# Linear attention whose matmuls all use TensorE tiles of 64 rows by 128 columns, on one Trainium2 core

## The chip, the cores and the metric

The kernel runs on one core of one Trainium2 chip. The core has TensorE (PE, with its weight loads shown apart as PEld), VectorE (DVE), ScalarE (ACT), GpSimd (POOL) and SyncE (SP, which here only issues DMAs). The metric is the time of one execution on the device in microseconds; less is better.

## The reference

Attention with exponential features for 8 batches of 8 heads, 576 tokens each, head size 64, followed by a mixture of experts (MoE) over the 4608 tokens. All is float32.

```python
def phi(x):
    proj = np.einsum('bhsd,df->bhsf', x, w_phi)                      # 128 features
    proj = proj - np.max(np.abs(proj), axis=-1, keepdims=True)
    return np.concatenate([np.exp(proj), np.exp(-proj)], axis=-1)    # 256 features
q_p, k_p = phi(q), phi(k)
kv  = np.einsum('bhsf,bhsd->bhfd', k_p, v)
z   = np.sum(k_p, axis=2)
num = np.einsum('bhsf,bhfd->bhsd', q_p, kv)
den = np.einsum('bhsf,bhf->bhs', q_p, z)[..., None] + 1e-06
x   = (num / den).transpose(0, 2, 1, 3).reshape(B * S, H * D)        # 4608 x 512
# MoE: logits = x @ w_gate; experts of equal capacity are filled in order of the logits;
# out[its tokens] = relu(x @ w1[e]) @ w2[e], for 8 experts, hidden size 1024
```

## The kernel before

Attention goes over 16 units, each two batches by two heads: 18 chunks of 128 tokens of one head, 9 for each of the two heads `a`. The two batches lie one behind the other, so of the 9 chunks four belong to the first batch, four to the second, and the one between them (`s_ == 4`, `j == 4`) is half and half. A unit's steps have names that the planner and this text use:

- `ld`: SyncE loads `ki`, `qi`, `vi` (L106 to L122), two to three units ahead.
- `kt`, `qt`: TensorE transposes k and q, 128 by 128 (L165, L243); ScalarE copies them out of PSUM (`kh`, `qh`).
- `kg`, `qg`: the projection on `w_phi` (`project`, L152), in tiles of 64 by 64: three groups of 12 matmuls for k and three for q. VectorE takes the largest absolute value of each token (`km`, `qm`, L156) and subtracts it (`kt`, `qtt`, L159). For k, ScalarE takes the two exponentials (`kP`, L177 and L178). For q, TensorE first transposes the difference (`T`, L255), so that features stand on partitions; then ScalarE takes the exponentials (`qP`, L258).
- `kv`: v stands still, `kP` moves, 64 columns by 256 features (L189, L194). GpSimd adds up `kP` over chunks (`ad`, L201 to L205), and TensorE sums that over tokens against a column of ones (`z`, L234).
- `bd`: the result is copied to `kvT` and multiplied by a block-diagonal matrix `bd` that holds a unit matrix and the gate weights (L222). This gives `kz`: per feature 64 columns of key-value, 8 of key-value times gate, and one for the key sum.
- `num`: `qP` stands still in tiles of 128 rows by 64 columns, `kz` moves, 73 columns (L279). VectorE adds 1e-6 to the denominator, inverts it, multiplies the 8 gate columns (`lg`, L288) and the 64 others (`xp`, L298). `xp` is stored to `xs` in DRAM, and the logits pile up in `L`.

At the end of each batch pair (every fourth unit) VectorE also does a first part of the routing (`pr`), and TensorE a count (`cnt`). After attention comes the routing, then the experts, whose rows are gathered from `xs`.

The order on each engine is written by the class `Plan`. Every step is an entry with an engine, a duration in ns, a due time, the steps it depends on, and claims on buffers (`slot`); PE steps also carry the tile shape (`mode`: A 128 by 128, B 128 by 64, Q 64 by 64). `order` repeatedly takes the engine's cheapest candidate; the resulting order is fixed, and each engine works through its own in order. In PSUM, two tiles `D` of two banks each serve `kg`, `qg`, `T` and `bd`; two tiles `S` of one bank serve `kt`, `qt`, `z`, `num` and `cnt`; two banks belong to `kv`.

Of the kernel before, what the change touches and what calls it, by code (L numbers as in the profile page):

```python
# [17 lines left out]
class Plan:  # L18
# [3 lines left out]
    SEM=40.; dl=0.; wp=6.  # L22
# [5 lines left out]
    def order(self):  # L28
# [7 lines left out]
        while left:  # L36
            best=None; horizon={}
            cand={}
            for x in left:
                e=x['eng']  # L40
                if len(cand.get(e,()))>=40: continue
                r=x['after']
                ok=x['seq'] is None or 'start' in self.by[x['seq']]
                if not ok: continue
                for d_ in x['deps']:
                    y=self.by[d_]
                    if 'end' not in y: ok=False; break
# [25 lines left out]
            if e=='PE':  # L73
                m0=x['mode'][0]
                if mode[0] not in (None,m0): s+=95.
                if mode[0]!=m0 or s>free.get(e,0.)+1.: s+=100. if m0=='A' else 50.
# [13 lines left out]
def attention(ctx, tc, nc, q, k, v, w_phi, w_gate, xs, L, C, xp, cfg={}, after=None, later=None, count=None, init=iter(())):  # L90
# [3 lines left out]
    d=dict(TI=21.,kt=-4.,kg=0.,kv=4.,bd=4.,z=5.,zc=6.,qt=6.,qg=10.,T=2.5,num=26.,stay=2.,ks=4.,qs=4.,ns=5.,ng=6,ld=60.,nqP=8,init=25.,pitch=1.)  # L94
# [7 lines left out]
    p=ps.tile([128,512],F32,name='S0',bufs=1)  # L102
    for _ in range(cfg.get('nwarm',7)): PE.matmul(p,w[:,0:128],w,start=True,stop=True)
    T={}
    HS=S*D
    def load(u,first=lambda: None):  # L106
        bp,hp=divmod(u,NP)
        qi=sb.tile([128,2,9,D],F32,name='qi',bufs=2); ki=sb.tile([128,2,9,D],F32,name='ki',bufs=2); vi=sb.tile([128,2,9,D],F32,name='vi',bufs=3)
        T['q',u],T['k',u],T['v',u]=qi,ki,vi
        def put(t,p,s0,s1,x,b,row):  # L110
# [22 lines left out]
    KV=(((0,0),(1,5),(0,1),(1,6),(0,2),(1,7),(0,3),(1,8)),((0,9),(1,14),(0,10),(1,15),(0,11),(1,16),(0,12),(1,17)))  # L133
    dv=lambda n,ps_=True: (150 if ps_ else 110)+1.03*n-95
    ac=lambda n,ps_=True: (170 if ps_ else 200)+.83*n-100
    QI=227.
    def unit(u):
        bp,hp=divmod(u,NP)
        t0=u*d['TI']
        def add(name,eng,dur,due,fn,deps=(),mode=None,slot=(),frees=(),lat=None,after=0.):  # L140
            P.add((name,u),eng,dur,t0+due,fn,[(x,u) for x in deps],
                  lat={'PE':170.,'DVE':95.,'ACT':100.,'POOL':30.,'SP':0.}[eng] if lat is None else lat,mode=mode,slot=slot,frees=frees,after=after)
        add('ld','SP',600. if u else 0.,-d['ld'],lambda x: load(u) if u else None,slot=(('qi',2,('qi',u)),('ki',2,('ki',u)),('vi',3,('vi',u))),lat=4500. if u else 0.)
        def slots(*l): return tuple((kd,n,(kd,u) if len(z)==0 else (kd,u)+tuple(z)) for kd,n,*z in l)
        ld0=('ld',)

        def project(x,X,src,i0,i1):
            p=X['p']=bank(X['b'],[128,2,512])(x)
            for i in range(i0,i1):
                for c in range(2):  # L150
                    for r in range(2):
                        PE.matmul(p[64*(c^r):64*(c^r)+64,r,128*(i-i0):128*(i-i0)+128],src[64*r:64*r+64,i,64*(c^r):64*(c^r)+64],C['w'][64*r:64*r+64,:],start=True,stop=True,skip_group_check=True)  # L152
# [8 lines left out]
        for g in range(3):  # L161
            def pe(x,g=g):
                if g==0: T['kh',u]=sb.tile([128,9,128],F32,name='kh',bufs=2)
                p=T['ktp',u,g]=bank(('S',u,'kt',g),[128,3,128])(x)
                for i in range(3): PE.transpose(p[:,i],ch(T['k',u],3*g+i),ident)  # L165
            def act(x,g=g): A.copy(T['kh',u][:,3*g:3*g+3],T['ktp',u,g])
            due=d['kt']+d['ks']*1.5*g
            add(('kt',g),'PE',327.,due,pe,ld0,'A',slots(('S',NS,'kt',g),*((('kh',2),) if g==0 else ())),(('ki',u),),after=(5500.,9000.,10000.)[g] if u==0 else 0.)
            add(('kh',g),'ACT',ac(384),due+.4,act,(('kt',g),),frees=(('S',u,'kt',g),))
        for g in range(3):  # L170
# [12 lines left out]
        for g in range(2):
            def pe(x,g=g):
                kP=T['kP',u]; v_=T['v',u]
                if g==0: T['kvps',u]=[ps.tile([128,256],F32,name='kv%d'%i,bufs=1) for i in range(2)]
                for i,b in KV[g]:
                    a,s_=divmod(b,9); c=a^i
                    PE.matmul(T['kvps',u][i][64*c:64*c+64,:],v_[:,a,s_,:],kP[:,b,:],start=b in (0,5,9,14),stop=False,skip_group_check=True)  # L189
                if g==1:  # L190
                    for a in range(2):
                        for i in range(2):
                            c=a^i; r=slice(64*i,64*i+64)
                            PE.matmul(T['kvps',u][i][64*c:64*c+64,:],v_[r,a,4,:],kP[r,9*a+4,:],start=False,stop=True,skip_group_check=True)  # L194
            add(('kv',g),'PE',4*430.+(530. if g==1 else 0.),d['kv']+d['ks']*(2+2.5*g),pe,[('ke',1+g)]+([('kv',0)] if g else []),('B','Q') if g else 'B',slots(('kv',1)) if g==0 else (),(('kP',u),('vi',u)))
        def ad(a,i):
            def f(x):
                kP=T['kP',u]
                if a==0 and i==0: T['ks',u]=sb.tile([128,2,2,256],F32,name='ks',bufs=2)
                ks=T['ks',u]; X=lambda s_: kP[:,9*a+s_:9*a+s_+6:5]  # L200
                if i==0: G.tensor_add(ks[:,:,a],X(0),X(1))  # L201
                elif i<3: G.tensor_add(ks[:,:,a],ks[:,:,a],X(i+1))  # L202
# [12 lines left out]
        def bdp(x):
# [674 lines left out]
```

## Time and profile before

| what | us |
|---|---|
| runs (median; all) | 858.12; 858.25, 856.98, 858.12 |
| the profiled execution | 857.9 |
| its span, first to last instruction | 856.1 |
| TensorE busy in the span | 803.4 |
| VectorE busy | 570.2 |
| ScalarE busy | 370.0 |
| GpSimd busy | 262.1 |

```profile
PEclk9999999999999999958999999999999999999999
```

The last line cuts the span into 40 slices of 21.4 us and gives the granted TensorE clock in tenths; it is full but for two slices behind the end of attention, where the routing keeps TensorE idle. A row of a timeline is start, length, engine, line, operation, output and inputs, tile (rows\*columns), moving operand, count, and in brackets the idle time before it with what ended it. A row of groups ends in the busy time, the mean ns of one, and the idle time before them. A row of stretches is the stretch, its length, the busy time of PE, PEld, DVE, ACT and POOL, the granted clock, the DMA share and GB/s.

### The profile page before, as it was taken

How to read it: one execution, taken by the hardware profiler on the slowest of the kernel's cores; microseconds unless marked ns; L12 is line 12 of the kernel's file. 1: busy time of each engine (PE TensorE's matmuls, PEld its weight loads, DVE VectorE, ACT ScalarE, POOL GpSimd, SP SyncE). 2: the span in 40 equal slices, each digit the busy share in tenths (PEclk: the TensorE clock that was granted, in tenths of full speed). 3: DMA queues.
4: the chain of work that ended last, by engine and by line, in shares of the span. 5: the costliest groups of instructions: out<-in, count | busy, mean ns of one | idle time of the engine just before them, and what ended most of it. 6: DMA issues, size and time to landing. Idle time of an engine off the chain costs nothing.

```text
span 856.1 us, 24776 instructions
## 1 busy us (share of the span) xinstructions
PE 803.4 (94%) x10508; PEld 685.8 (80%) x10508; DVE 570.2 (67%) x1534; ACT 370.0 (43%) x691; POOL 262.1 (31%) x300
## 2 busy tenths in 40 slices
PE   4879999999999999758999999999999999999995
PEld 2768887887788878658979879889889798898984
DVE  1787788778867887577858658668667577461410
ACT  1646665566566565413334324333333243251410
POOL 1654455555555555111040130310301202401001
PEclk9999999999999999958999999999999999999999
DMA  8424444454445421134143340532233225610301
GB/s 170 116 54 113 114 114 126 118 135 121 117 120 134 117 58 31 57 114 131 54 147 118 129 147 35 177 131 95 97 118 123 83 104 185 214 63 38 118 13 43
DMA packets 73534, 91.88 MB, mean 107 GB/s; under 512 B 5280, under 2 KB 56512, under 8 KB 73424
## 3 DMA queue, kind: packets, MB, share of 16 engines
q1 hardware_dynamic: 67328, 71.32, 29.3%
q0 software_dynamic: 6096, 18.98, 6.5%
q8 instruction: 83, 1.36, 0.7%
q14 instruction: 27, 0.22, 0.1%
HBM read 71.40 MB, written 18.87 MB: 105 GB/s over the span
## 4 chain that ended last, share of the span: by engine, by line
PE 69%; issue 16%; DVE 7%; POOL 4%; DMA 2%; ACT 1%; SPq 0%; POOLq 0%; DVEq 0%; ACTq 0%
PE h L763 19%; PE y L792 16%; PE S L279 7%; PE D L152 6%; PE kv L189 4%; PE D L255 3%; PE y L807 2%; PE S L165 2%; PE S L243 2%; PE h L739 2%; PE S L234 2%; DVE km L156 1%; PE rps L530 1%; POOL out_dram L821 1%; DVE kt L159 1%
## 5 line engine op out<-in xcount | busy, mean ns | idle before, releaser
L763 PE MATMUL h<-xh,w1h 128*128 128x272 f32 (+1 forms) x512 | 145.9, 305 | 0.7 <-ACT xh L740 0.7
L763 PE MATMUL h<-xh,w1l 128*128 128x304 f32 (+1 forms) x512 | 143.9, 301 | 0.0
L774 ACT ACTIVATE fh<-h 128x272 fp32r<-128x272 f32 (+1 forms) x128 | 49.2, 384 | 134.5 <-PE h L763 122.1
L821 POOL DMA_INDIRECT out_dram<-ysb,idx x40 | 40.5, 1012 | 207.0 <-ACT ysb L815 203.5
L792 PE MATMUL y<-w2h,fl 128*128 128x512 f32 x256 | 102.0, 398 | 0.0
L792 PE MATMUL y<-w2l,fh 128*128 128x512 f32 x256 | 101.9, 398 | 0.0
L792 PE MATMUL y<-w2h,fh 128*128 128x512 f32 x256 | 101.5, 396 | 0.0
L763 PEld LDWEIGHTS h<-xh,w1h 128*128 128x128 f32 x512 | 97.2, 190 | 2.5 <-issue 1.2
L763 PEld LDWEIGHTS h<-xh,w1l 128*128 128x128 f32 x512 | 97.4, 190 | 0.0
L734 POOL DMA_INDIRECT xg<-xs,idx x40 | 40.0, 1000 | 178.2 <-issue 141.5
L763 PE MATMUL h<-xl,w1h 128*128 128x272 f32 (+1 forms) x512 | 91.4, 298 | 0.0
L778 DVE SCALAR_TENSOR_TENSOR fl<-h,fh 128x272 fp32r<-128x272 f32 (+1 forms) x128 | 52.8, 419 | 55.6 <-ACT fh L774 41.9
L201 POOL TENSOR_TENSOR ks<-kP 128x512 f32<-128x512 f32 x32 | 40.9, 1277 | 157.1 <-issue 130.2
L279 PE MATMUL S<-kz,qP 128*64 128x73 f32 x2304 | 87.4, 230 | 1.0 <-ACT xp L296 1.0
L279 PEld LDWEIGHTS S<-kz,qP 128*64 128x64 f32 x2304 | 78.1, 137 | 11.0 <-issue 9.1
L202 POOL TENSOR_TENSOR ks<-ks,kP 128x512 f32<-128x512 f32 x64 | 81.5, 1273 | 4.9
L258 ACT ACTIVATE qP<-D 128x768 f32<-128x768 f32 x96 | 72.5, 808 | 9.1 <-PE D L255 5.6
L763 PEld LDWEIGHTS h<-xl,w1h 128*128 128x128 f32 x512 | 75.5, 188 | 0.0
L815 ACT COPY ysb<-y 128x512 f32<-128x512 f32 (+1 forms) x40 | 21.8, 544 | 104.4 <-PE y L792 72.3
L156 DVE TENSOR_REDUCE km<-D 128x6 f32<-128x768 f32 x48 | 45.7, 953 | 29.4 <-PE D L152 29.2
L189 PE MATMUL kv<-kP,vi 128*64 128x256 f32 x512 | 60.9, 379 | 0.0
L156 DVE TENSOR_REDUCE qm<-D 128x6 f32<-128x768 f32 x48 | 45.6, 950 | 20.0 <-PE D L152 19.8
(177 smaller groups left out, 1550.5 us busy)
## 6 DMA issues: line engine op xcount, KB each, us to landing
raww<-in_moe_w_dram SPq DMA_DIRECT2D x64, 512.0 KB, 5.5
qi<-in_q_dram SPq DMA_DIRECT2D x32, 288.0 KB, 4.6
xs<-xp SPq DMA_DIRECT2D x16, 576.0 KB, 3.8
ki<-in_k_dram SPq DMA_DIRECT2D x32, 160.0 KB, 3.8
vi<-in_v_dram SPq DMA_DIRECT2D x32, 160.0 KB, 5.2
ki<-in_k_dram SPq DMA_DIRECT2D x32, 128.0 KB, 3.7
vi<-in_v_dram SPq DMA_DIRECT2D x32, 128.0 KB, 5.0
xg<-xs,idx POOLq DMA_INDIRECT x40, 3.5
```

Of the source, the lines that this page charges most:

```text
L152: PE.matmul(p[64*(c^r):64*(c^r)+64,r,128*(i-i0):128*(i-i0)+128],src[64*r:64*r+64,i,64*(c^r):64*(c^r)+64],C['w'][64*r:64*r+64,:],start=True ...
L156: V.tensor_reduce(m[:,:,0:n],X['v'],axis=AX.X,op=OP.max,apply_absolute_value=True)
L189: PE.matmul(T['kvps',u][i][64*c:64*c+64,:],v_[:,a,s_,:],kP[:,b,:],start=b in (0,5,9,14),stop=False,skip_group_check=True)
L201: if i==0: G.tensor_add(ks[:,:,a],X(0),X(1))
L202: elif i<3: G.tensor_add(ks[:,:,a],ks[:,:,a],X(i+1))
L258: for fh in range(2): A.activation(qP[:,fh].rearrange('p (b i) f -> p b (i f)',b=2),X['T'][:,:,0:384],AF.Exp,scale=1.0-2*fh)
L279: PE.matmul(p[64*ab:64*ab+64,j-j0,:],T['qP',u,jj][:,fh,o,64*ab:64*ab+64],T['kz',u][:,ab,fh,a^ab,:],start=fh==0,stop=fh==1)
L763: PE.matmul(p,ws[:,k,o:o+128],xx[:,k,o1:o2],start=n==0,stop=n==11)
L774: A.activation(hh[:,f,o1:o1+m1],p[:,0:m1],AF.Relu)
L778: V.scalar_tensor_tensor(hl[:,f,o1:o1+m1],p[:,0:m1],0.0,hh[:,f,o1:o1+m1],op0=OP.max,op1=OP.subtract)
L792: PE.matmul(p,hx[:,f,o:o+128],ws[:,f%2,:],start=n==0,stop=n==23)
L821: st=G.indirect_dma_start(out=ov,out_offset=bass.IndirectOffsetOnAxis(ap=iv,axis=0),in_=yv,in_offset=None)
```

## The change

All of attention's matmuls and transposes take tiles of 64 rows by 128 columns; two such tiles (`r` = 0 and 1, rows 0 to 63 and 64 to 127) write to two different PSUM banks.

- `project`: a chunk takes two matmuls instead of four.
- `turn` replaces the 128 by 128 transposes of k, q and the difference by two of 64 rows and 64 moving columns each. k and q come in groups of 3 and 6 chunks.
- `kv`: `kP` stands still (128 features), and `v1`, v with a column of ones, moves (65 columns); the key sum is the 65th column, so `ad` and `z` go. GpSimd makes `v1` (`vc`). The halves of the tokens land in two banks: ScalarE copies the first to `kz` (`kc`), VectorE adds the second (`kd`).
- The gate columns: both heads' key-value is transposed (`kT`, 4 pairs), copied, and multiplied by the gate weights `gw` (`gt`, 8 matmuls of 8 columns); VectorE copies the result to `kz` (`zk`).
- `num`: the sum over 128 feature rows is split over two banks. ScalarE copies bank 0 to `nu` (`xc`), VectorE adds bank 1 (two additions where the group has the mixed chunk, whose product is 146 columns wide), then as before, on `nu` in SBUF. The multiplication of the 64 columns goes to GpSimd (`xa`), in the last unit too, where ScalarE did it.
- All PSUM tiles of attention come from one ring of four tiles of two banks.
- q is laid out like k and v, in four loads instead of two, each of k, q and v has a planner entry of its own, and the rows of `xs` are stored by four DMAs instead of one; the table of token numbers follows (four iotas for one).
- The planner counts several claims of one kind, and a table `off` sets the due time of each step (`o0` and `oL` shift those of the first and last unit).

```diff
-                for c in range(2):
-                    for r in range(2):
-                        PE.matmul(p[64*(c^r):64*(c^r)+64,r,128*(i-i0):128*(i-i0)+128],src[64*r:64*r+64,i,64*(c^r):64*(c^r)+64],C['w'][64*r:64*r+64,:],start=True,stop=True,skip_group_check=True)
+                for r in range(2): PE.matmul(p[:,r,128*(i-i0):128*(i-i0)+128],src[64*r:64*r+64,i,:],C['w'][64*r:64*r+64,:],start=True,stop=True,skip_group_check=True)
...
+    ND_=4
+    def bank(u_):
+        return lambda x: ps.tile([128,2,512],F32,name='D%d'%x['buf'][u_],bufs=1)
+    def turn(p,n,f):
+        for i in range(n):
+            for r in range(2): PE.transpose(p[:,r,64*i:64*i+64],f(i)[64*r:64*r+64,:],ident[64*r:64*r+64,64*r:64*r+64])
...
+        def vcopy(x):
+            v1=T['v1',u]=sb.tile([128,2,9,D+1],F32,name='v1',bufs=2)
+            for a in range(2):
+                G.tensor_copy(v1[:,a,:,1-a:D+1-a],T['v',u][:,a])
+                G.memset(v1[:,a,:,a*D:a*D+1],1.0)
...
+                def mm(i,f,s_,r,stop):
+                    h=slice(64*r,64*r+64); n=(D+1)*(2*i+f)
+                    PE.matmul(p[:,r,n:n+D+1],kP[h,9*a+s_,128*f:128*f+128],v1[h,a,s_,:],start=r not in seen,stop=stop,skip_group_check=True); seen.add(r)
+                for f in range(2):
+                    for i in range(2):
+                        for s_ in range(5*i,5*i+4):
+                            for r in range(2): mm(i,f,s_,r,r!=i and s_==5*i+3)
+                    for i in range(2): mm(i,f,4,i,True)
+            def act(x,a=a):
+                if a==0: T['kz',u]=sb.tile([128,4,146],F32,name='kz',bufs=2)
+                A.copy(T['kz',u][:,:,8+65*a:73+65*a],T['kvps',u,a][:,0,0:4*D+4].rearrange('p (k n) -> p k n',n=D+1))
+            def dve(x,a=a):
+                z=T['kz',u][:,:,8+65*a:73+65*a]
+                V.tensor_add(z,z,T['kvps',u,a][:,1,0:4*D+4].rearrange('p (k n) -> p k n',n=D+1))
+            due=d['kv']+d['ks']*(2+2.5*a)
+            add(('kv',a),'PE',18*122.,due,pe,[('ke',1+a),('vc',)]+[('kv',0)]*a,'Q',slots(('D',ND_,'kv',a)),(('kP',u),('v1',u)))
...
+        def gate(x):
+            p=T['gp',u]=bank(('D',u,'gt'))(x)
+            for k in range(4):
+                for a in range(2): PE.matmul(p[:,a,8*k:8*k+8],T['kvT',u][64*a:64*a+64,k],C['gw'][64*a:64*a+64,2*hp+a],start=True,stop=True,skip_group_check=True)
+        add(('gt',),'PE',4*115.,kend+2.5,gate,[('kTc',)],'Q',slots(('D',ND_,'gt')))
...
-                            for ab in range(2):
-                                jj,o=divmod(9*a+j,6)
-                                PE.matmul(p[64*ab:64*ab+64,j-j0,:],T['qP',u,jj][:,fh,o,64*ab:64*ab+64],T['kz',u][:,ab,fh,a^ab,:],start=fh==0,stop=fh==1)
+                            for r in range(2):
+                                e=slice(64*r,64*r+64)
+                                PE.matmul(p[:,r,m:m+w],T['qP',u,jj][e,fh,o,:],T['kz',u].rearrange('p (i f) n -> p i f n',f=2)[e,i,fh,73*a:73*a+73],start=fh==0,stop=fh==1,skip_group_check=True)
+                def half(x,n=n,g=g,X=X):
+                    X['t']=sb.tile([128,6,73],F32,name='nu',bufs=3); w=73*n+73*(1-g)
+                    A.copy(X['t'].rearrange('p j n -> p (j n)')[:,0:w],X['p'][:,0,0:w])
...
-                    V.tensor_scalar(rd[:,:n],p[:,:n,72:73],1e-6,None,op0=OP.add)
+                    V.tensor_add(f,f,X['p'][:,1,0:73*n])
+                    if g==0: V.tensor_add(t[64:128,4],t[64:128,5],X['p'][64:128,1,365:438])
+                    rd=X['rd']=sb.tile([128,5,1],F32,name='rd',bufs=4)
+                    V.tensor_scalar(rd[:,:n],t[:,:n,8+56*a:9+56*a],1e-6,None,op0=OP.add)
...
-                    V.tensor_mul(lg[:,j0:j1,:,h],p[:,:n,64:72],rd[:,:n].to_broadcast([128,n,8]))
+                    V.tensor_mul(lg[:,j0:j1,:,h],t[:,:n,65*a:65*a+8],rd[:,:n].to_broadcast([128,n,8]))
...
+                    G.tensor_mul(x_[:,j0:j1,64*a:64*a+64],X['t'][:,:n,9-9*a:73-9*a],X['rd'][:,:n].to_broadcast([128,n,64]))
...
+ATT = {'TI': 22.027, 'kt': -4.44, 'kg': -1.69, 'kv': 7.48, 'bd': 4.17, 'z': 4.87, 'qt': -1.35, 'qg': 6.68, 'T': 12.67, 'num': 33.16, 'stay': 38.714, ... 'off': {('ld', 'k'): -82.61, ('ld', 'q'): -39.19, ...
```

What TensorE does in a row, in a steady unit before (output, then moving and standing operand, then the tile's rows or columns of output by moving columns, and the count):

```order
L279 MATMUL S_2561<-kz,qP 64x73 x20
L152 MATMUL D_2583<-w,qh 64x128 x12
L222 MATMUL D_2604<-bd,kvT 64x72 x16
L234 MATMUL S_2623<-one,ks 64x1 x16
L152 MATMUL D_2644<-w,kh 64x128 x12
L165 MATMUL S_2658<-ident,ki 128x128 x3
L243 MATMUL S_2664<-ident,qi 128x128 x3
L255 MATMUL D_2669<-ident,qtt 128x128 x6
L279 MATMUL S_2679<-kz,qP 64x73 x16
L152 MATMUL D_2699<-w,kh 64x128 x12
L152 MATMUL D_2720<-w,qh 64x128 x12
```

And now, in a steady unit, where the gate stands between key-value and numerator:

```order
L196 MATMUL D_2051<-v_1297,kP 128x65 x36
L154 MATMUL D_2099<-w,kh 128x128 x6
L272 MATMUL D_2113<-kz,qP 128x73 x16
L272 MATMUL D_2113<-kz,qP 128x146 x4
L216 MATMUL D_2143<-ident,kz 128x64 x8
L127 MATMUL D_2154<-ident,qtt 128x64 x12
L154 MATMUL D_2176<-w,kh 128x128 x6
L223 MATMUL D_2185<-gw,kvT 128x8 x8
L272 MATMUL D_2197<-kz,qP 128x73 x16
L272 MATMUL D_2221<-kz,qP 128x73 x16
L272 MATMUL D_2221<-kz,qP 128x146 x4
L154 MATMUL D_2252<-w,qh 128x128 x6
```

The rows of three shapes became rows of one; `bd` and `z` (L222, L234) are gone, `kT` and `gt` (L216, L223) are new, and every output is a tile of the one ring `D`.

VectorE in the same place before, from the key sum's copy on:

```order
L235 COPY kz<-S_1514 128x8
L156 TENSOR_REDUCE km<-D_1535 128x6
L159 TENSOR_TENSOR kt<-D_1535,km 128x2x3x128
L283 TENSOR_SCALAR rd<-S_1570 128x4
L284 RECIPROCAL rd<-rd 128x4
L288 TENSOR_TENSOR lg<-S_1570,rd 128x32
L298 TENSOR_TENSOR xp<-S_1570,rd 128x4x64
L156 TENSOR_REDUCE km<-D_1590 128x6
L156 TENSOR_REDUCE qm<-D_1611 128x6
L159 TENSOR_TENSOR kt<-D_1590,km 128x2x3x128
L159 TENSOR_TENSOR qtt<-D_1611,qm 128x2x3x128
```

And now:

```order
L207 TENSOR_TENSOR kz<-kz,D_1644 128x4x65
L158 TENSOR_REDUCE km<-D_1692 128x6
L161 TENSOR_TENSOR kt<-D_1692,km 128x2x3x128
L278 TENSOR_TENSOR nu<-nu,D_1706 128x365
L279 TENSOR_TENSOR nu<-nu,D_1706 64x73
L281 TENSOR_SCALAR rd<-nu 128x5
L282 RECIPROCAL rd<-rd 128x5
L286 TENSOR_TENSOR lg<-nu,rd 128x40
L158 TENSOR_REDUCE km<-D_1768 128x6
L225 COPY kz<-D_1777 128x4x8 x2
L161 TENSOR_TENSOR kt<-D_1768,km 128x2x3x128
```

The multiplication to `xp` is gone; an addition of 365 or 292 and one of 73 stand ahead of `rd`, which with `lg` reads `nu` in SBUF; `kz` takes two additions and two gate copies in a unit.

SyncE's first loads before:

```order
L113 DMA ki<-in_k_dram 64x2x320
L113 DMA ki<-in_k_dram 64x2x256
L113 DMA ki<-in_k_dram 64x2x320
L113 DMA ki<-in_k_dram 64x2x256
L113 DMA qi<-in_q_dram 64x2x576 x2
L113 DMA vi<-in_v_dram 64x2x320
L113 DMA vi<-in_v_dram 64x2x256
```

And now:

```order
L114 DMA ki<-in_k_dram 64x2x320
L114 DMA ki<-in_k_dram 64x2x256
L114 DMA ki<-in_k_dram 64x2x320
L114 DMA ki<-in_k_dram 64x2x256
L114 DMA ki<-in_k_dram 64x2x320
L114 DMA ki<-in_k_dram 64x2x256
L114 DMA ki<-in_k_dram 64x2x320
L114 DMA ki<-in_k_dram 64x2x256
L114 DMA qi<-in_q_dram 64x2x320
L114 DMA qi<-in_q_dram 64x2x256
```

The second unit's k stands ahead of the first unit's q and v.

More of the change, by code (lines that the diff above doesn't have):

```diff
@@ L74, in order @@
                 m0=x['mode'][0]
[L75 to L76 removed]
+                if mode[0] not in (None,m0): s+=self.swc
+                if mode[0]!=m0 or s>free.get(e,0.)+1.: s+=self.swA if m0=='A' else self.swO
                 mode[0]=x['mode'][-1]
@@ L101, in attention, with load, put @@
     w=sb.tile([128,512],BF,name='warm',bufs=1); V.memset(w,0.0)
-    p=ps.tile([128,512],F32,name='S0',bufs=1)
-    for _ in range(cfg.get('nwarm',7)): PE.matmul(p,w[:,0:128],w,start=True,stop=True)
+    p=ps.tile([128,2,512],F32,name='D0',bufs=1)
+    for _ in range(cfg.get('nwarm',7)): PE.matmul(p[:,0],w[:,0:128],w,start=True,stop=True)
     T={}
     HS=S*D
[L106 to L110, printed above, removed]
+    def load(u,n,first=lambda: None):
+        bp,hp=divmod(u,NP); b=2*bp
+        x=dict(q=q,k=k,v=v)[n]
+        t=T[n,u]=sb.tile([128,2,9,D],F32,name=n+'i',bufs=3 if n=='v' else 2)
+        def put(p,s0,s1,b,row):
             n=s1-s0
@@ L183, in unit @@
[L183 to L195, printed above, removed]
@@ new lines, in unit, with kT, kTc @@
+        kend=d['kv']+4*d['ks']
+        def kT(x):
+            p=T['kTp',u]=bank(('D',u,'kT'))(x)
+            for k in range(4):
+                for r in range(2): PE.transpose(p[:,r,64*k:64*k+64],T['kz',u][64*r:64*r+64,k,9:137],ident[64*r:64*r+64,64*r:64*r+64])
+        def kTc(x):
+            t=T['kvT',u]=sb.tile([128,4,128],F32,name='kvT',bufs=2)
+            A.copy(rows(t),halves(T['kTp',u],4))
+        def gate(x):
+            p=T['gp',u]=bank(('D',u,'gt'))(x)
+            for k in range(4):
+                for a in range(2): PE.matmul(p[:,a,8*k:8*k+8],T['kvT',u][64*a:64*a+64,k],C['gw'][64*a:64*a+64,2*hp+a],start=True,stop=True,skip_group_check=True)
@@ L241, in pe, with act @@
                 if g==0: T['qh',u]=sb.tile([128,9,128],F32,name='qh',bufs=2)
-                p=T['qtp',u,g]=bank(('S',u,'qt',g),[128,3,128])(x)
-                for i in range(3): PE.transpose(p[:,i,:],ch(T['q',u],3*g+i),ident)
-            def act(x,g=g): A.copy(T['qh',u][:,3*g:3*g+3],T['qtp',u,g])
+                p=T['qtp',u,g]=bank(('D',u,'qt',g))(x)
+                turn(p,i1-i0,lambda i: ch(T['q',u],i0+i))
+            def act(x,g=g,i0=i0,i1=i1): A.copy(rows(T['qh',u][:,i0:i1]),halves(T['qtp',u,g],i1-i0))
```

179 lines of the change are left out of this document (73 added, 106 removed).

## The prediction

> **What bounds the kernel now.** I read the page first, then the busy time by stretch, then TensorE's timeline of one steady unit, then the waits of VectorE.
>
> ```profile
> span 856.1 us, 24776 instructions
> PE 803.4 (94%) x10508; PEld 685.8 (80%) x10508; DVE 570.2 (67%) x1534; ACT 370.0 (43%) x691; POOL 262.1 (31%) x300
> 61.29:327.35 266.06, 260.03 (x5598) 216.89 (x5592) 211.04 (x453) 165.71 (x274) 137.44 (x130) 1.00 0.44 112
> 345.42 1.10 PE L234 MATMUL S<-one,ks 128*64 128x1 f32 x32
> 348.98 2.51 PE L279 MATMUL S<-kz,qP 128*64 128x73 f32 x72
> 352.47 2.50 PE L279 MATMUL S<-kz,qP 128*64 128x73 f32 x72 [0.99 <-ACT xp L296]
> 357.81 0.70 PE L469 MATMUL rps<-OH,cmp 128*32 128x8 bf16 x9 [2.83 <-DVE OH L460]
> ```
>
> The third line is the busy time from the key sum (L234) of the second unit to that of the fifteenth: length, then PE, PEld, DVE, ACT and POOL, then the granted clock (full), the DMA share and GB/s. Those 13 units take 20.47 us each, and TensorE is busy for 260.03 of 266.06 us. The sixteenth key sum starts at 345.42, the last attention product ends at 354.97, and routing starts at 357.81. So attention is the first 42% of the span, it is bound by TensorE, and all that follows is untouched but for a table of token numbers. Only attention can gain or lose.
>
> ```profile
> 160.49 1.49 PE L279 MATMUL S<-kz,qP 128*64 128x73 f32 x40
> 161.90 0.89 PE L152 MATMUL D<-w,qh 64*64 64x128 f32 x24
> ...
> 164.25 0.89 PE L152 MATMUL D<-w,kh 64*64 64x128 f32 x24
> 165.06 0.55 PE L165 MATMUL S<-ident,ki 128*128 128x128 f32 x3
> ...
> 167.69 0.89 PE L152 MATMUL D<-w,kh 64*64 64x128 f32 x24
> 168.39 0.83 PE L152 MATMUL D<-w,qh 64*64 64x128 f32 x24
> 169.16 1.49 PE L279 MATMUL S<-kz,qP 128*64 128x73 f32 x40
> 170.48 1.90 PE L189 MATMUL kv<-kP,vi 128*64 128x256 f32 x16
> ...
> 172.69 0.82 PE L255 MATMUL D<-ident,qtt 128*128 128x128 f32 x6
> 173.35 0.49 PE L165 MATMUL S<-ident,ki 128*128 128x128 f32 x3
> ...
> 180.19 1.49 PE L279 MATMUL S<-kz,qP 128*64 128x73 f32 x40
> ```
>
> Starts are what to read here, since ends overlap. A unit without the extra work of a batch pair's end runs from 160.49 to 180.19, 19.70 us. Followed by its own tile shape, a projection of 24 takes 0.70 (167.69 to 168.39); followed by another shape it takes 0.77 or 0.81. A numerator of 40 takes 1.32 before the same shape and 1.41 before another. So a change of shape costs 0.07 to 0.11 us, and this unit has 13 of them.
>
> **The change on TensorE, per unit.** All attention matmuls now have 64 rows and 128 columns, so the 13 changes go. A record below is one half of an f32 matmul: the trace has 40 where the code issues 20. Two records on different tiles run together; the 72 numerator records in 2.51 us (last one 0.23) are 36 pairs, 0.0633 us a pair of 73 columns.
> - Projections: 6 groups as before at 0.70, 4.20 us.
> - Transposes: 9 for k, 9 for q, 18 for the exponent's argument, and 4 new ones for the gate, each as two halves of 64 columns. Six whole ones took 0.66 (172.69 to 173.35), 0.110 each. If halves run together a pair costs 0.063, if in turn 0.110; I take 0.110, as nothing in before shows two transposes side by side: 40 x 0.110 = 4.40.
> - Key-value: 72 pairs of records of 65 columns at 0.0633, 4.56. These replace kv, the block-diagonal product and the key sum.
> - Gate: 4 times 2 matmuls, 8 pairs, 0.51.
> - Numerator: 64 pairs at 0.0633 and 8 of 146 columns at twice that, 5.06.
>
> The sum is 18.73 us against 19.70.
>
> The unknown is the weight load. Stationary tiles get 128 columns instead of 64.
>
> ```profile
> L763 PEld LDWEIGHTS h<-xh,w1l 128*128 128x128 f32 x512 | 97.4, 190 | 0.0
> L279 PEld LDWEIGHTS S<-kz,qP 128*64 128x64 f32 x2304 | 78.1, 137 | 11.0 <-issue 9.1 <-ACT xp L296 1.1 <-ACT kh L166 0.5
> L739 PEld LDWEIGHTS h<-ident,xg 64*128 64x128 f32 x32 | 2.7, 143 | 2.2 <-issue 1.8 <-DVE xl L741 0.4
> ```
>
> The last number ahead of the second bar is the mean of one in ns. In the expert layers 128 columns load in 190 ns, 53 more than 64 columns. In the one place with the new tile shape (64*128, a transpose) they load in 143, 6 more. By the second a pair stays near 0.063; by the first it becomes 0.116 wherever fewer than 128 columns stream. I take the second: it has the very tile shape, and the planner's entries in the diff (18*122 ns for a key-value group, 4*115 for the gate) would be off by half otherwise, while those before agree with the trace (4*430 = 1720 for a kv group that starts 1.83 us before what follows it). No time is taken from those entries. The row that speaks against it is an ordinary matmul's, so this stays a rival.
>
> The Trainium skill, "TensorE: Matmul & The Clock Gate", section "LDWEIGHTS (loading the stationary operand)", says that a load takes the number of its columns divided by 1.2 ns, whatever its rows. The 53 ns between the first two rows agree with it and the 143 of the third does not. By the rule the unit would be about 25 us, an estimate (107 ns a pair), and the kernel some 80 us slower.
>
> **The change on VectorE, per unit.**
>
> ```profile
> DVE qm L156 <- PE D L152: 15.9, 10, 1.8
> DVE rd L283 <- PE S L279: 15.7, 23, 0.8
> DVE km L156 <- PE D L152: 12.6, 17, 1.8
> L298 DVE TENSOR_TENSOR xp<-S,rd 128x320 f32<-128x320 f32 x26 | 12.5, 481 | 0.0
> L298 DVE TENSOR_TENSOR xp<-S,rd 128x256 f32<-128x256 f32 x26 | 10.8, 414 | 0.0
> 198.15 0.99 DVE L293 SCALAR_TENSOR_TENSOR L<-L,lg 128x32 f32<-128x32 f32 x1
> 121.03 0.23 DVE L293 SCALAR_TENSOR_TENSOR L<-L,lg 128x40 f32<-128x40 f32 x1
> 196.44 2.62 POOL L202 TENSOR_TENSOR ks<-ks,kP 128x512 f32<-128x512 f32 x2
> ```
>
> In the 266 us VectorE waited for TensorE 44.2 us in these three rows (three smaller waits make it 47), so it is taken for 219, 16.85 us a unit. The two multiplications differ by 67 ns for 64 elements: 1.05 ns an element. What goes: the four `xp` multiplications, which move to GpSimd, and the copy of the key sum. What comes: per head an addition of 365 (0.528) and one of 73 (0.22), and one of 292 (0.45), on which the reciprocal then waits, where the multiplication that goes had nobody behind it. With 0.09 of overlap off what went (0.39 and 0.33), that is +0.48 a head, +0.96. The two halves of key-value add 0.35 each, +0.70, and the gate's second copy +0.1. Together 18.6 us, as much as TensorE's 18.73: the cover under which VectorE's work was free is gone.
>
> ScalarE has 165.71/13 = 12.75 us a unit; it copies one bank of each sum, some 1.3 us more net at 0.48 for 384 elements, and stays below. GpSimd loses the key sums (137.44/13 = 10.6) and gets four multiplications of 256 or 320 elements (two additions of 512 took 2.62, so 0.66 and 0.82) and two copies of 576 of at most 1.5 each: under 6. The store waits for GpSimd now, four transfers for one; on the queue 12 loads and 4 stores at 0.68 (2.72 for four, below) are 10.9 us of a unit, and loads run ahead by two buffers, so I cost it at nothing. PSUM becomes one ring of four two-bank tiles for 21 claims a unit; a claim that waits for VectorE stops TensorE behind it.
>
> **The sum.** Per unit: 18.73, plus what units have now over 19.70 (20.47 - 19.70 = 0.77, mostly batch ends), plus 0.3 for TensorE waiting on a VectorE that is 95% taken (0.47 a unit idle now, (266.06 - 260.03)/13, with 82% taken). That is 19.8 for 20.47, -0.67. From 61.29 to 345.42 are 14 units, so -9.4; the two units at the start are costed with it.
>
> ```profile
> 0.77 2.72 SPq L113 DMA_DIRECT2D ki<-in_k_dram  x4
> 3.53 1.26 SPq L113 DMA_DIRECT2D qi<-in_q_dram  x2
> 15.64 0.66 PE L165 MATMUL S<-ident,ki 128*128 128x128 f32 x2 [6.00 <-DMA ki<-in_k_dram]
> 18.96 0.96 DVE L156 TENSOR_REDUCE km<-D 128x6 f32<-128x768 f32 x1 [14.60 <-PE D L152]
> ```
>
> At the start the third k transpose waits for k until 15.64, since q and v are issued right behind it, and VectorE first has work at 18.96. After the change the second unit's k comes behind the first's, half the bytes of q and v. Bounds: nothing, to the 9 us from 6.9 (its first piece) to 15.64; I take -4, since what then limits is VectorE. At the end a copy, an addition and the small one stand between the last product and routing (0.45 + 0.53 + 0.22, with hand-overs 1.5). So 857.9 - 9.4 - 4 + 1.5 = 846.0; the profiled execution took 857.9, 0.2 below the median, so **846 us**.
>
> **Rivals.**
> - VectorE becomes the bound, slower. Where GpSimd works, an operation of VectorE on two SBUF operands waits for its instruction to end: L293 took 0.99 while L202 ran, 0.23 else. `rd` and `lg` now read SBUF instead of PSUM. If one of them is caught in each of the four groups at 0.6, VectorE needs 18.6 + 2.4 = 21.0, and 14 x (21.0 - 20.47) - 4 + 1.5 makes 863. It decides from 20.47 - 18.6 = 1.9 us of such waits a unit. Against it: GpSimd's busy time halves, and its multiplication follows the group it belongs to. The Trainium skill, "SBUF — State Buffer", section "SBUF: two separate sides", calls it an exclusive lock, held for the whole instruction; by it the PSUM additions are spared, and L293 agrees.
> - Loads bind: the pairs at 0.116 make 72 x 0.116 + 8 x 0.116 + 64 x 0.116 + 1.01 + 8.6 = 26.3 us a unit, 6.6 over 19.70, and in 16 units +106: about 960.
> - The gain does not come: waits in the ring eat the 13 changes and the start is bound by VectorE as now. Then only the 1.5 at the end is left: about 859.
> - Halves of transposes run together: TensorE falls by 40 x 0.047 = 1.9, VectorE binds at 18.6 + 0.5 = 19.1, and with the whole 9 us of the start it is 857.9 - 14 x 1.37 - 9 + 1.5 = 831.
>
> **How the numbers follow.** Forecast 0.62 (833 to 856), the transposes' case 0.05, no gain 0.06, VectorE 0.17, loads 0.10. The range 832 to 868 leaves out the loads, half the transposes' case and a little above 868: under 0.2. Runs of this kernel lie 0.15% apart, so 0.2% counts as no change. Faster 0.67, same 0.06, slower 0.27.
>
> **What would show it.** TensorE's groups: `kv` near 2.3 us by starts and the gate near 0.5; twice that means loads. VectorE's L278 near 530 ns, and `rd` and `lg` at 157 and 232 unless GpSimd catches them. A unit of 19 to 20 us between gate products. Waits of TensorE on `nu` or `kz` by VectorE would show the ring. First `km` before 16 us. I am wrong on the sign if VectorE's idle time in the steady part nears zero with a unit above 20.5.

## The result, and the profile after

The changed kernel takes 950.25 us (median of 952.59, 958.57, 939.21 and 947.92) against 858.18: 1.103 times as long (95% interval 1.093 to 1.113). Ratios leave out executions more than 1.5% above their kernel's fastest, here 958.57. The forecast was 846, with 960 for the rival in which weight loads bind.

The page of the changed kernel, its first lines, the clock by slices (each 23.8 us), and the loads of the two large products:

```profile
span 950.8 us, 25778 instructions
PE 904.3 (95%) x10956; PEld 836.0 (88%) x10956; DVE 594.2 (62%) x1616; ACT 389.1 (41%) x705; POOL 158.4 (17%) x271
PEclk8999999989997999955579999999999999999999
L272 PEld LDWEIGHTS D<-kz,qP 64*128 64x128 f32 x2304 | 150.2, 207 | 4.7 <-DVE qtt L161 1.8 <-issue 1.3 <-PE D L272 0.7
L196 PEld LDWEIGHTS D<-v,kP 64*128 64x128 f32 x2304 | 139.8, 198 | 0.1
```

TensorE is 101 us busier with 448 instructions more, PEld 150 us busier. A load of a numerator takes 207 ns on average where it took 137, and a key-value load 198, stretches at half clock included. Behind its first slice the clock row has three dips, the last from slice 18 to 21; before had one, after attention.

One steady unit of TensorE, from gate product to gate product (what is left out is transposes and projections):

```profile
210.63 1.06 PE L223 MATMUL D<-gw,kvT 64*128 64x8 f32 x16
211.54 4.32 PE L272 MATMUL D<-kz,qP 64*128 64x73 f32 x72
215.70 0.83 PE L154 MATMUL D<-w,qh 64*128 64x128 f32 x12
216.37 0.54 PE L127 MATMUL D<-ident,qtt 64*128 64x64 f32 x12
216.74 4.19 PE L196 MATMUL D<-v,kP 64*128 64x65 f32 x72
220.76 0.89 PE L154 MATMUL D<-w,qh 64*128 64x128 f32 x12
...
234.96 1.06 PE L223 MATMUL D<-gw,kvT 64*128 64x8 f32 x16
```

By starts, 36 pairs with 65 moving columns take 4.02 us, 0.112 a pair; 8 pairs with 8 columns take 0.91, 0.114; the first numerator 4.16, 0.116 a pair (four of its 36 move 146 columns). Between 8 and 73 moving columns the time hardly changes. Six pairs of transposes take 0.37, 0.062 a pair. The unit is 24.33 us where the one shown of before had 19.70.

The end of attention, TensorE and then the busy time of the stretch (length, PE, PEld, DVE, ACT, POOL, granted clock, DMA share, GB/s), with a steady stretch ahead of it:

```profile
399.87 1.26 PE L154 MATMUL D<-w,qh 64*128 64x128 f32 x12 [1.20 <-DVE qtt L161]
400.86 15.52 PE L196 MATMUL D<-v,kP 64*128 64x65 f32 x144
...
425.74 1.88 PE L223 MATMUL D<-gw,kvT 64*128 64x8 f32 x16
427.41 19.32 PE L272 MATMUL D<-kz,qP 64*128 64x73 f32 x176
450.73 0.70 PE L467 MATMUL rps<-OH,cmp 128*32 128x8 bf16 x9 [4.00 <-DVE OH L458]
```

```profile
208.00:284.00 76.00, 75.42 (x1419) 74.55 (x1418) 55.64 (x128) 43.07 (x71) 12.20 (x24) 1.00 0.36 98
397.00:450.00 53.00, 47.61 (x463) 47.31 (x461) 17.75 (x62) 11.14 (x20) 5.40 (x8) 0.53 0.08 22
```

TensorE works through these products without a gap and yet at half the clock: 144 records take 15.26 us by starts (0.212 a pair). Routing starts at 450.73 instead of 357.81, 92.9 later. Up to the second unit (gate product 55.63, key sum before 61.29) 5.7 us are won; the 14 units to the sixteenth (425.74) take 370.1 instead of 284.1, +86.0; from there to routing it is 25.0 instead of 12.4, +12.6.

### The profile page after: what moved, and what is told of

Its sections match the earlier page's. It is cut to its first block, busy times and chain, and to the rows that moved or that the text cites. A ratio compares the mean times of both kernels' runs of the same rounds, so it can differ in the third digit from the quotient of the medians.

```text
span 950.8 us, 25778 instructions
## 1 busy us (share of the span) xinstructions
PE 904.3 (95%) x10956; PEld 836.0 (88%) x10956; DVE 594.2 (62%) x1616; ACT 389.1 (41%) x705; POOL 158.4 (17%) x271
## 4 chain that ended last, share of the span: by engine, by line
PE 79%; issue 11%; DVE 4%; POOL 2%; ACT 1%; DMA 1%; SPq 0%; POOLq 0%; ACTq 0%; DVEq 0%
PE h L761 17%; PE D L272 16%; PE y L790 14%; PE D L196 14%; PE D L154 7%; PE D L127 3%; PE y L805 2%; PE D L223 2%; PE h L737 2%; PE rps L528 1%; POOL out_dram L819 1%; PE rps L524 1%; DVE qtt L161 1%; DVE qm L158 1%; DMA ki<-in_k_dram 1%
## 5 line engine op out<-in xcount | busy, mean ns | idle before, releaser
L272 PE MATMUL D<-kz,qP 64*128 64x73 f32 (+1 forms) x2304 | 157.0, 294 | 2.9 <-DVE qtt L161 1.4
L272 PEld LDWEIGHTS D<-kz,qP 64*128 64x128 f32 x2304 | 150.2, 207 | 4.7 <-DVE qtt L161 1.8
L196 PE MATMUL D<-v,kP 64*128 64x65 f32 x2304 | 141.4, 281 | 0.0
L196 PEld LDWEIGHTS D<-v,kP 64*128 64x128 f32 x2304 | 139.8, 198 | 0.1
L295 POOL TENSOR_TENSOR xp<-nu,rd 128x320 f32<-128x320 f32 x64 | 43.3, 677 | 301.1 <-DVE rd L282 274.1
L275 ACT COPY nu<-D 128x438 f32<-128x438 f32 (+1 forms) x64 | 29.7, 464 | 91.8 <-PE D L272 87.2
L278 DVE TENSOR_TENSOR nu<-nu,D 128x365 f32<-128x365 f32 x64 | 31.6, 494 | 50.4 <-ACT nu L275 50.2
```

The costliest lines, as they stand in the source:

```text
L196: PE.matmul(p[:,r,n:n+D+1],kP[h,9*a+s_,128*f:128*f+128],v1[h,a,s_,:],start=r not in seen,stop=stop,skip_group_check=True); seen.add(r)
L272: PE.matmul(p[:,r,m:m+w],T['qP',u,jj][e,fh,o,:],T['kz',u].rearrange('p (i f) n -> p i f n',f=2)[e,i,fh,73*a:73*a+73],start=fh==0,stop=fh== ...
L278: V.tensor_add(f,f,X['p'][:,1,0:73*n])
L295: G.tensor_mul(x_[:,j0:j1,64*a:64*a+64],X['t'][:,:n,9-9*a:73-9*a],X['rd'][:,:n].to_broadcast([128,n,64]))
```

## Experiments

**Shapes by themselves.** The theory is that the load of an ordinary f32 matmul costs by its columns, is not covered by fewer than about 128 moving columns, and that the two row tiles do load side by side.

```python
def pairs(c,N=48):
    p=bank()
    for i in range(N):
        for r in range(2): PE.matmul(p[:,r,0:c],S[64*r:64*r+64,:],M[64*r:64*r+64,0:c],**kw)
...
for m in (0,2,6):                          # m vector operations in the pause
    p=tall(512,60); pause(p,m)             # 128x128 tiles, 512 moving columns
    p=pairs(65,500); pause(p,m)
    p=pairs(128,500); pause(p,m)
    ...                                    # 450 times four 64x64 quadrants
```

> This kernel leaves the whole computation out; it only issues stretches of equal TensorE matmuls with nothing to wait for, on all 512 columns at first, then one shape after another, then long stretches of one shape with a pause ahead of each. Theory A (the load of the stationary tile sets the time, by its columns): pairs of 64-row tiles with 128 stationary columns take 0.112 us a pair at 8, 33, 65, 73 and 100 moving columns, then grow (128: 0.12, 200: about 0.19); a single row tile alone takes about the same 0.11 per record; four 64x64 quadrants take about 0.06 for 65 columns; 128x64 column pairs about 0.06; 128x128 with 65 columns about 0.11. Theory B (the two row tiles do not run beside each other): one row tile alone takes 0.056 per record, and the quadrants 0.11 or more for four. Theory C (writing two banks of PSUM in turn): 128x128 at 65 columns falls with the pairs, and one row tile into one bank takes half a pair. On the clock: if a load-bound stretch streams too little to earn the full clock, the pairs of 65 columns after a pause stay at 0.21 us a pair for tens of us, while the 512-column stretch and the 128-column pairs return to full within 10 us; if only the pause matters, all return alike.

TensorE's timeline of it, at full clock where not said otherwise, and one row of busy time (here length, PE, PEld, DVE, POOL, then the clock):

```profile
235.84 6.03 PE L68 MATMUL b<-M,S 128*64 128x65 f32 x192
241.80 21.70 PE L52 MATMUL b<-M,S 128*128 128x65 f32 x192
263.43 3.25 PE L72 MATMUL b<-I,S 64*128 64x64 f32 x96
266.52 10.88 PE L75 MATMUL b<-I,S 64*128 64x64 f32 x192
277.24 1.62 PE L78 MATMUL b<-MB,SB 64*128 64x65 bf16 x96
332.81 111.88 PE L48 MATMUL b<-M,S 64*128 64x65 f32 x2000 [0.81 <-DVE S L42]
445.50 111.94 PE L48 MATMUL b<-M,S 64*128 64x128 f32 x2000 [0.81 <-DVE S L42]
565.46 2.09 PE L89 MATMUL b<-M,S 64*64 64x65 f32 x128 [1.67 <-issue]
1105.26 213.38 PE L48 MATMUL b<-M,S 64*128 64x65 f32 x2000 [3.58 <-DVE S L42]
1322.21 114.39 PE L48 MATMUL b<-M,S 64*128 64x128 f32 x2000 [3.57 <-DVE S L42]
33.00:67.00 34.00, 34.00 (x346) 33.43 (x346) 0.00 (x0) 0.00 (x0) 0.56 0.01 1
```

A pair with 65 columns and a pair with 128 take the same 0.112 us. Tiles of 128 by 128 take it too, one record each (241.80 to 263.43; 96 records with 65 columns, 96 with 128). A single row tile that writes to one bank takes 0.11 a record (14 records in 1.67 us from 163.57, the last one 0.22), so it is neither the two banks nor the row tiles taking turns. Four quadrants go through in 0.059 (15 ns a record within a burst), 128-by-64 pairs in 0.062. Up to 128 moving columns, what sets the time is the number of stationary columns; 96 pairs with 146 moving columns take 12.1 us and with 200 16.4, where 0.112 a pair would be 10.8. A transpose (L72) is one record and its pair takes 0.064; an ordinary f32 matmul of the same tile and columns (L75) is two records, and each pair of those takes 0.112: a transpose's load does not tell what an f32 matmul's costs. In bf16 the same pair takes 0.032.

Three things came unasked. The quadrants stop after each 128 records with no wait but "issue" (none that the profile shows), so their mean is 28 to 29 ns a record instead of 15. And after a pause of 3.58 us the 65 columns stay at half clock for all of 213 us, while 128 columns return to the full one. Third, the clock also falls without any wait. The last row holds pairs of 8 and then 33 columns, and TensorE is busy in all 34.00 us; the clock is 0.95 from their start at 33.57 to 37.57, and from there to 115, with pairs of 65 and 73 columns behind, 0.50. So these widths were measured at half clock here, where 96 pairs with 33 columns and 96 with 73 take 20.7 us alike.

**Key-value alone in quadrants.** Each stationary tile is split into two of 64 columns.

```diff
-PE.matmul(p[:,r,n:n+D+1],kP[h,9*a+s_,128*f:128*f+128],v1[h,a,s_,:],...)
+for c in range(2):
+    PE.matmul(p[64*c:64*c+64,r,n:n+D+1],kP[h,9*a+s_,128*f+64*c:128*f+64*c+64],v1[h,a,s_,:],...)
```

> The key-value products alone go from two 64x128 tiles to four 64x64 quadrants (twice the instructions, the same sums and banks). Theory A (load by its columns): a step of 65 columns falls from 0.112 to 0.062 us, the group of x72 from 4.0 to 2.2 to 2.3 us, the unit by about 3.5 us from 24.33 to 21, and the run from 950 to 890 to 900 us. Theory B (row tiles one after the other) and theory C (two banks): no gain, 950 to 1000 us, since there are twice as many records.

```profile
213.26 2.59 PE L197 MATMUL D<-v,kP 64*64 64x65 f32 x144
215.78 0.94 PE L154 MATMUL D<-w,kh 64*128 64x128 f32 x12
```

903.18 us: 1.054 of the kernel before (1.047 to 1.061), 47 less than the change and 3 above its range. Twice the records take 2.52 us instead of 4.02 (2.26 in most other groups, as expected). The unit is 23.4 on average (56.53 to 383.75, 14 units) where about 21 was expected. Of the 51 us by which routing starts earlier (399.41), 23 lie behind the fifteenth gate product (360.08, in the change 388.63), where the change runs mostly at half clock; so the sum came out near the forecast partly by luck.

**The numerator alone in quadrants**, in the same way.

> The numerator alone goes from two 64x128 tiles to four 64x64 quadrants. Theory A: a step of 73 columns falls from 0.116 to about 0.07 us, the 146-column ones stay at 0.12 to 0.14, the unit falls by about 2.9 us to 21.4, the run from 950 to 900 to 910 us. Theories B and C: 950 to 1000 us.

907.57 us, 1.057 (1.054 to 1.060), 43 less, in its range. Both gain, as the load theory alone expected; serial rows and the two banks are out.

**More columns for the same loads.** The pairs of the numerator stream 120 columns; what is surplus is overwritten or not read, for which one head's chunks run in reverse order.

```diff
-w=146 if j==4 else 73
+w=146 if j==4 else 120
```

> The numerator's 64 pairs with 73 moving columns stream 120 columns instead, the 47 others being overwritten or not read; the loads are unchanged. Load theory: the pairs stay at 0.116 us, the unit at 24.3 to 24.6 us, and the run at 940 to 955 us; if moreover the clock is held down because load-bound stretches stream too little, the last numerators (x176, 19.3 us) fall to about 11 and the run to 925 to 940. Rival (the time goes by moving columns, 0.116 for 73): 64 x 0.07 = 4.8 us a unit more, 1020 us.

```profile
232.99 1.06 PE L223 MATMUL D<-gw,kvT 64*128 64x8 f32 x16
233.90 4.67 PE L274 MATMUL D<-kz,qP 64*128 64x120 f32 x72
238.37 0.86 PE L154 MATMUL D<-w,qh 64*128 64x128 f32 x12
...
396.14 15.53 PE L196 MATMUL D<-v,kP 64*128 64x65 f32 x144
...
419.68 10.19 PE L274 MATMUL D<-kz,qP 64*128 64x120 f32 x176
```

The 72 records take 4.47 us, as the same group does in the changed kernel's next unit (235.88 to 240.35), and a unit 24.36 (208.63 to 232.99). Sixty-four per cent more columns in 32 of these 36 pairs cost nothing. The run takes 935.31 us, 1.090 (1.088 to 1.091): 15 less than with 73 columns. At the end the key-value products (still 65 columns) sit at half clock for their 15.53 us as in the changed kernel, but the wider numerators behind them bring the clock back: the last 176 records take 10.19 us instead of 19.32.

**All three products in quadrants.**

> Key-value, gate and numerator in 64x64 quadrants; the token tile that two batches share takes 73 columns from each batch's own half instead of 146, and its extra addition on VectorE goes. From the two parts alone (950 to 903 and to 907.5): the load theory says that they add up, 950 - 47 - 43 - 7 for the gate = 853 us, the unit 24.3 - 3.4 - 2.8 - 0.4 = 17.7 us of TensorE, so VectorE (about 17 us a unit) comes close to being the bound and the forecast is 845 to 865. If the gains don't add, because the waits on VectorE or the supply of instructions (fourfold records, gaps of 1.5 us after each 128) take the place of the loads, 870 to 885.

It took 913.57 us, 1.064 (1.062 to 1.065), more than either part alone. The lower case was wrong and even the higher too low. TensorE's longest waits between 55 and 380 us, and the longest for VectorE (total, times, longest):

```profile
PE D L276 <- issue: 27.9, 28, 2.3
PE D L197 <- issue: 18.1, 16, 1.9
PE D L127 <- DVE qtt L161: 2.7, 2, 1.4
```

With 762 records a unit in the trace (456 in the changed kernel) they come at 32.4 ns each from the second to the sixteenth gate product, near the 28 to 29 of the quadrants by themselves. All rows with "issue" make 57.5 us, all with VectorE 4.4: the supply of instructions has taken the place of the loads, and the waits on VectorE have not.

**Between the two: the numerator in quadrants for one head only.**

> The changed kernel with key-value in quadrants and the numerator in quadrants for one head of each pair: 672 matmul records a unit, between the 600 of either part alone and the 762 to 790 of all. Theory (the supply of instructions bounds all in quadrants: 29 ns a record): 672 x 0.029 = 19.6 us a unit, TensorE's own sum is 20.5 - 1.4 = 19.1, so the two nearly meet and the run is faster than either part alone: 885 to 898 us. Rival (VectorE and its waits bound the quadrants, not the supply): 903 to 915, as the others, and no idle time of TensorE put down to issue.

906.07 us, 1.058 (1.054 to 1.062): no gain over key-value alone, a miss for the theory's number, which lies in the rival's range. But TensorE's idle time by "issue" between 55 and 380 us, which the rival excluded, rose from 7 us (key-value alone) to 19. That is over half of the 22 us expected (16 times 1.4); the rest isn't accounted for. Perhaps an average below the limit does not help while the quadrants come in bursts; no run tests it.

**The clock, by width.** After 70 matmuls of 512 columns and a pause, 300 pairs of one width.

> This kernel leaves the whole computation out: 70 matmuls of 512 columns at full clock, a wait of TensorE for VectorE, then 300 pairs of 64x128 tiles of one width, seven times: 65 columns after about 2.2, 2.6 and 3.5 us, then 96, 112, 120 and 128 columns after 3.5 us. Theory (the clock comes back only while the array streams for most of the time): 65 columns stay at 0.21 us a pair to the end of the stretch, 128 return to 0.112 within 10 us, and the limit lies between; with a shorter wait the clock never falls. Rival (the clock comes back by the time the array is occupied, and the one stretch seen at half clock was an accident): all return within 10 us.

```profile
70.39 127.00 PE L48 MATMUL b<-M,S 64*128 64x65 f32 x1200 [2.10 <-DVE S L42]
649.21 70.22 PE L48 MATMUL b<-M,S 64*128 64x96 f32 x1200 [3.58 <-DVE S L42]
1049.66 67.27 PE L48 MATMUL b<-M,S 64*128 64x128 f32 x1200 [3.58 <-DVE S L42]
75.00:195.00 120.00, 120.00 (x1128) 120.00 (x1128) 0.00 (x0) 0.00 (x0) 0.50 0.01 1
```

The last row is busy time as in the first of these kernels: TensorE is busy for 120.00 of 120.00 us and the clock is 0.50. With 65 columns it never comes back; with 96 and more it does within 7 us. "With a shorter wait the clock never falls" held behind 512 columns for 0.81 and 1.73 us in that first kernel, not for 2.10 here. Behind pairs of 65 columns, 1.73 us was enough there (clock 0.50 from 829.80 to 832, 1.00 from 836), so the length of the wait does not decide by itself.

**The routing steps spread out.** At a pair's end they are due further apart, and the count behind them moves along.

```diff
-t0+d['num']+25+i*d.get('prs',.7)
+t0+d['num']+25+i*d.get('prs',2.)
```

> The changed kernel with the twelve routing steps at the end of each pair of batches due 2 us apart instead of 0.7, so that VectorE isn't late for TensorE there; nothing else moves. Clock theory (the half clock begins behind those waits of 1.7, 0.9 and 1.2 us and is kept by load-bound work): the waits go, with them the stretches at half clock from 195, 298 and 400 us, and the run falls from 950 to 915 to 930 us, with units at 24.3 to 25.1 throughout. Rival (the clock falls for another reason, for instance for the share of streaming alone): the stretches stay and the run is at 940 to 952 us.

```profile
PEclk9999999999999999995699999999999999999998
416.60 0.70 PE L467 MATMUL rps<-OH,cmp 128*32 128x8 bf16 x9 [4.61 <-DVE OH L458]
```

925.03 us, 1.077 (1.071 to 1.083), 24 less than the change by the means behind the ratios (922.8 and 946.6). In the profiled execution (918.27) attention runs at the full clock from 13 us to its end and every unit from 54.86 to 400.07 takes 23.4 to 26.0 us. Routing starts at 416.60, 34 earlier. Other executions of it still lose clock (granted 0.963 in one of 931.22, 0.946 in one of 940.00), so the waits are a cause of the fall, but not the only one; above, it fell without any.

**Parts of the change put into the kernel before.** First the 64-row transposes of the query alone, then the early keys alone, then both.

```diff
-for i in range(6): PE.transpose(p[:,i//3,128*(i%3):128*(i%3)+128],t[:,i],ident)
+for i in range(6):
+    for r in range(2): PE.transpose(p[:,r,64*i:64*i+64],t[64*r:64*r+64,i],ident[64*r:64*r+64,64*r:64*r+64])
```

> The kernel before with one part of the change alone: the query's second transposes (x6 of 128x128, 0.65 us from start to start) become x12 of 64x128 in pairs, into two banks; ScalarE's two exponentials read the reordered columns. Where the prediction was wrong the other way, a pair of such transposes took 0.062 us, so a group takes 0.37: 3 x 0.28 = 0.84 us a unit less and two shape changes a group fewer (about 0.08 each), 16 units: 858 to 840 to 847 us. Rival: VectorE (16.9 us a unit, and late for the transposes in several places) takes the gain: 853 to 858.

> The kernel before with one part of the change alone: the second unit's keys are loaded right behind the first's, ahead of the first queries and values. From the pair of runs with and without it on the 64-row transposes (856.45 and 850.59) this is worth 5.9 us by itself: 851 to 854 us. Rival: it pays only beside the 64-row transposes: 856 to 859.

> The same, and the keys of the second unit are loaded right behind those of the first, ahead of the first queries and values, as the changed kernel does (there the first maximum began at 11.40 us against 18.96). Theory: the wait of 6.0 us for the keys goes and the fill shortens by 4 to 6 us beside the gain of the transposes: 835 to 842 us. Rival: the queries and values are then late, or the fill is set by something else: as without it.

The transposes alone give 856.45 us, 0.998 (0.997 to 0.999); the keys alone 853.63, 0.994 (0.992 to 0.996); both 850.59, 0.991 (0.989 to 0.993), the shortest here. The keys' expectation held. The transposes' was missed, with a time in the rival's range, and so was that of both together, because the transposes give 0.2% instead of 1.3 to 2.1. TensorE's timeline with the transposes alone:

```profile
218.26 0.55 PE L243 MATMUL S<-ident,qi 128*128 128x128 f32 x3
218.73 0.59 PE L256 MATMUL D<-ident,qtt 64*128 64x64 f32 x12
219.26 0.55 PE L165 MATMUL S<-ident,ki 128*128 128x128 f32 x3
```

The group takes 0.53 by starts where six whole ones took 0.66, but the 128-row transposes on both sides, which had stood beside their own shape, now take 0.47 each (0.38 and 0.42 in the same place before): 1.47 for the three groups instead of 1.46. TensorE's waits for VectorE between 55 and 350 us are 4.1 us, 3.9 before. So the two changes of shape took the gain, not the rival's VectorE.

**Supply and shape changes by themselves.**

> This kernel leaves the whole computation out. 450 steps of four 64x64 quadrants (3600 records) run once on a quiet chip and once while SyncE's queue moves 28 MB of weights in: the theory that the supply of instructions bounds the all-quadrants kernel expects 28 to 29 ns a record quiet (102 us, bursts of 128 records and gaps of 1.5 us) and more beside the transfers, 31 to 36 ns, which is what that kernel ran at (32.4); the rival, that the kernel's 32 ns came from VectorE, expects no difference. Then 240 whole transposes of 128x128, 240 pairs of 64x128, and both in turns by six: if a change between 128-row and 64-row tiles costs 0.1 us or more, the turns take 0.2 us more a round than the two alone (0.11 and 0.062 each, 1.03 us a round); if not, 1.03. Last, 40 pairs of 64x128 and 40 steps of quadrants, and both in turns by four: the same between 64-row tiles of 128 and of 64 columns.

```profile
85.14 2.09 PE L60 MATMUL b<-M,S 64*64 64x65 f32 x128 [1.64 <-issue]
88.59 2.09 PE L60 MATMUL b<-M,S 64*64 64x65 f32 x128 [1.36 <-issue]
215.81 3.74 PE L60 MATMUL b<-M,S 64*64 64x65 f32 x128 [3.00 <-issue]
396.70 15.41 PE L66 MATMUL b<-I,S 64*128 64x64 f32 x480
412.04 0.88 PE L63 MATMUL b<-I,S 128*128 128x128 f32 x6
412.84 0.59 PE L66 MATMUL b<-I,S 64*128 64x64 f32 x12
413.36 0.88 PE L63 MATMUL b<-I,S 128*128 128x128 f32 x6
q8 instruction: 77, 1.26, 0.9%
```

Quiet, 128 records come every 3.45 to 4.00 us, 28.6 ns each over 25 bursts. Beside transfers of 348 GB/s it is 6.74 us, 53 ns each, well over the 31 to 36 expected. The clock was at half there too, but at half clock the records themselves need only 3.74; the 3.00 behind them are a wait for instructions. When the transfers end, 256 records take 7.18 us (248.98 to 256.16), 28 each, though the clock is at half until 254. The last row is a DMA queue of its own: 77 packets, 1.26 MB, 16 KB each, for 19,920 matmul records and loads of TensorE; in the first of these kernels it is 210 packets for 53,832. That is one packet for about 256, the 128 records of a burst with their loads. So transfers slow the supply; VectorE, which does nothing here, is not needed for it. Six whole transposes and six pairs in turns take 1.32 us a round; alone they take 0.110 and 0.064 each, 1.04. A change of shape costs 0.14. The last part, pairs and quadrants in turns, ran at half clock (0.50 from 505 to 520 us) and gives no price for the full one.

## Why the prediction was wrong

**The failed step is the weight load.** The prediction had two prices for a load of 128 columns, 190 ns from an ordinary matmul's row and 143 from the row with the very tile shape, a transpose, and took the second: 0.0633 us a pair. It measured 0.110 to 0.116. By starts in the unit shown, with its groups left out there, key-value is 7.99 us (4.56 forecast), the numerator 8.29 (5.06) and the gate 0.91 (0.51): 7.06 too much. The tile shape was right and the kind of instruction wrong; of the same tile and columns, the transpose's pair takes 0.064 and the f32 matmul's 0.112. The second reason for the choice, that the planner's entries would be off by half otherwise, was no evidence: they are off by half (18*122 ns is 2.2 us, for 4.02).

The Trainium skill, "TensorE: Matmul & The Clock Gate", section "LDWEIGHTS (loading the stationary operand)", gives 107 ns for 128 columns, and an estimate from it was some +80 us. The runs agree with it for f32 matmuls (112 ns a pair; 14 units at full clock cost +61 net, see below), not for transposes (64).

**Projections** were 4.32 a unit for 4.20, right. **Transposes** were missed the other way: halves run together, so all of them, with what hand-overs lie among them, take 2.82 instead of 4.40. With this the unit is 24.33 where the loads rival had 26.3 and the forecast 18.73 (19.8 with its waits). That 950 is so near the rival's 960 is luck in part: units 2 us shorter than the rival's make about -31 in 16, and the clock, which it didn't have, +33.

**The shape changes** cost what the prediction said or more (0.14 between whole and halved rows). By estimate the 13 that went are worth 0.9 to 1.8 us a unit (0.07 to 0.14 each); the loads, 7.06, took that several times over.

**The start** was right: 5.7 us gained up to the second unit, 4 forecast, and 5.1 by the early keys alone (858.70 to 853.63). **GpSimd** fell from 262.1 to 158.4 us. **VectorE** was near its forecast, busy 55.64 us in 76.00, 17.8 a unit for 18.6. Its groups of the changed kernel between 208 and 284 us (busy, mean ns, idle before):

```profile
L278 DVE TENSOR_TENSOR nu<-nu,D 128x365 f32<-128x365 f32 x7 | 3.7, 532 | 3.7 <-ACT nu L275 3.7
L286 DVE TENSOR_TENSOR lg<-nu,rd 128x40 f32<-128x40 f32 x6 | 1.4, 232 | 0.2
```

The addition takes 532 ns for 528 forecast, and `lg`, forecast at 232, isn't caught by GpSimd there. With units of 24.33 VectorE could not bind, so whether it would at 20 stays untested.

**The clock was not in the prediction.** With load-bound products TensorE is busy nearly all the time and still loses the clock behind short waits at a pair's end. Twice it gets it back within 7 to 10 us, with projections of 128 columns in between (clock 0.55 from 195 to 200 us, 0.76 to 205, then 1.00); at the end, where 144 load-bound records and then 176 come in a row, it doesn't. Against the execution that kept it, 14 units take 370.1 instead of 345.2 us (400.07 - 54.86), and the end 25.0 instead of 16.5: 33 us, with the waits ahead of the falls. So of the 92.9 by which routing starts later, -5.7 are the start, +61.1 the units at full clock (345.2 - 284.1; the loads, less what transposes and shape changes gave), +4.1 the longer end at full clock, and about +33.4 the clock, by these two executions.

## What to carry to other kernels

Price a weight load by a row of the same kind of instruction, not only of the same tile: for f32 matmuls it was the stationary columns, 0.112 us for 128, and moving fewer columns than that bought nothing. Splitting such a tile into quadrants gains until the instructions themselves come too slowly, so count records as well as time. A TensorE that is busy 100% of a stretch can still sit at half clock if it streams few columns; read the granted clock of each stretch before explaining its length.

## What the runs showed that was not expected

- After 512 columns and a wait of 2.1 us or more, pairs with 65 moving columns stay at half clock for as long as they ran (127 and 213 us) with TensorE busy throughout; 96 columns bring it back within 7 us. Pairs with 8 lose it without a wait. The Trainium skill, "TensorE: Matmul & The Clock Gate", section "What's actually happening", has the full clock return after one busy window of about 3.4 us; this disagrees with it, unless busy means streaming.
- Quadrants by themselves are limited to 28.6 ns a record by the supply of instructions, in bursts of 128, and to about 53 beside transfers of 348 GB/s.
- A bf16 pair with 64 rows, 128 stationary and 65 moving columns takes 0.032 us where f32 takes two records of 0.112 a pair.
